# Six one-bank PSUM tiles instead of three two-bank tiles in the last stage of an attention and feed-forward kernel

## Chip, cores and metric

The kernel runs on one core of a Trainium2 chip. The metric is the time of one execution on the device in microseconds (us), and smaller is better. The engines are named as in the profile: PE (TensorE, matrix products), PEld (its weight loads), DVE (VectorE), ACT (ScalarE), POOL (GpSimd) and SP (SyncE, which only issues transfers here).

## What is computed

The inputs are q, k and v of 8 batches, 12 heads, 448 rows and 64 columns, and two weight matrices of 768 x 3072 and 3072 x 768. The attention uses a squared relu in place of a softmax:

```python
scores = scale * np.matmul(q, k.transpose(0, 1, 3, 2))
attn = np.maximum(scores, 0.0) ** 2 / S
x = np.matmul(attn, v)                      # heads side by side: 8 x 448 x 768
mixed = np.real(fft(fft(x, axis=1), axis=2))
u = x + mixed
un = (u - mu) / np.sqrt(var + 1e-06)        # over the 768 columns
out = u + np.maximum(un @ w_ch1, 0.0) @ w_ch2
```

## The kernel before

The 8 x 448 = 3584 rows of `un` are cut into twelve groups for the feed-forward part: groups of 384, 512 and 384 rows and then nine of 256. While the attention and the Fourier mixing of later batches still run, the first eight groups go through the feed-forward one at a time, between the other work (`ffn`, L1874). The last four groups come after all other work, in two pairs (`JOINTS`, L216): `joint` (L1733) takes two groups of 256 rows together and forms their first product by seven block products in place of eight (a scheme of Strassen's kind over two row halves and two halves of the 768 inner columns). The stage of the change is these two joints; in the profile it runs from 451.4 us to the end.

In a joint there are twelve blocks (`i`), and each has seven block products on PE. One block product is three matmuls of 256 columns (`product`, L1757, matmul at L1762), in a half of one PSUM bank. Three generators per block say in which order they come:

- `main` (L1786) takes one bank. It makes a product there, ACT copies the bank to SBUF (`copy`, L1777), PE adds a second product to the same bank, ACT copies it again, PE adds a third, ACT copies again, PE adds a fourth, and ACT's relu (L1806) writes the result to `hB`.
- `second` (L1810) takes one bank and makes one product. DVE adds the first copy and applies the relu (`sum_out`, L1782) into `hT`.
- `third` (L1819) takes one bank and makes one product. DVE adds the third copy (L1782, into `hB`), PE adds a last product, and DVE adds the second copy (L1782, into `hT`).

So a bank goes back and forth between PE and its readers, ACT and DVE, while other blocks use the other banks. The second product of the feed-forward (`Pair`, L2018) is a chain of matmuls of 384 columns (L2071), between which DVE adds a bank to the row block that will be stored (`adder`, L1623).

The order of all work is written by a planner while the program is built (`Streams.run`, L102): each generator asks for an engine with a duration, times of its inputs and free buffers, and the planner takes the request that can start first. The order on each engine is then fixed, and each engine works through its own queue in that order. What an instruction waits for is not written in the kernel. The layer below the kernel keeps a record per tile, and puts semaphore waits where an instruction touches a tile that another engine has used.

PSUM has eight banks here. `BF` (L238) makes two tiles of one bank, named `psF`. `BS` (L237) makes three tiles of two banks each, named `psS`; the attention needs both banks of such a tile in one instruction, since ACT reads the scores of two heads together (L967). In the last stage `spread` (L1708) takes the three wide tiles for good and hands out their six halves as single banks; two more come from `BF`. The eight are the pool `B8`:

```python
tiles, plain = [BS.take() for _ in range(3)], []
B8 = Banks(6, lambda i: tiles[i // 2][:, i % 2] if i < 6 else plain[i - 6])
```

Of the kernel before, what the change touches and what calls it, by code (L numbers as in the profile page):

```python
# [10 lines left out]
FP32 = mybir.dt.float32  # L11
# [138 lines left out]
def need(eng, dur, deps=(), bufs=(), ok=None):  # L150
    return eng, dur, list(deps), list(bufs), ok


def mm(n):
    return n / 2400 + (0.002 if STAGE[0] else 0.006)
# [22 lines left out]
def kernel(  # L178
# [10 lines left out]
    B, H, S, Dh = q.shape  # L189
# [33 lines left out]
    wpool = ctx.enter_context(tc.tile_pool(name="w", bufs=1))  # L223
    work = ctx.enter_context(tc.tile_pool(name="work", bufs=1))
    psum = ctx.enter_context(tc.psum_pool(name="ps", bufs=1))
    dram = ctx.enter_context(tc.tile_pool(name="dr", bufs=1, space=bass.MemoryType.DRAM))


# [5 lines left out]
    nbot = [dram.tile([UB, D], BF16, name=f"nbot{b}") for b in range(B)]  # L234


    BS = Banks(3, lambda i: psum.tile([128, 2, 512], FP32, name="psS", tag=f"S{i}", bufs=1))  # L237
    BF = Banks(2, lambda i: psum.tile([128, 512], FP32, name="psF", tag=f"F{i}", bufs=1))  # L238
    sch = Streams()
    STAGE[0] = 1  # L240
# [161 lines left out]
    def halve():  # L402

        yield need("SP", 0.0, [tail_left])
        e = yield need("PE", mm(2 * SX), [], [BS])
        pt = BS.take()
        for t in range(2):
# [4 lines left out]
        nc.vector.tensor_copy(half_seq[0][:2 * EH], pt[:2 * EH, :, 0:2 * EV].rearrange("p t (s o) -> p t o s", o=2))  # L412
        BS.give(pt, e)
        BQR.free.append(e)
# [397 lines left out]
    def turned_for(b, i):  # L812

        g, r = divmod(i, 7)
        return turned_at[b][g] if r == 3 else [turned_at[b][g][r > 3]]
# [18 lines left out]
    def attention(b, left=None):  # L834
# [8 lines left out]
        while pv < MC:  # L843
# [18 lines left out]
            if values:  # L862
                deps += [sv[i][1] for i in items(mv)]
                if b > 1:
                    yield need("PE", 0.0, deps, [], gate)
                    if chains[0] == 2:
                        homes, n = BS, min(n, 2)
                bufs.append(homes)
# [5 lines left out]
            if n:  # L874
                now = sorted(range(p, p + n), key=lambda i: i % 7 == 3)
                deps += [c for i in now for c in turned_for(b, i)]
                bufs += [BS] * n
                last = [sum(1 + (j % 7 == 3) for j in now[x + 1:]) * mm(S) for x in range(n)]
# [6 lines left out]
            for part in ("scores", "values") if few else ("values", "scores"):  # L885
                if part == "values" and values:
                    held = homes.take()
                    av = held[:, 0] if homes is BS else held
                    give = lambda when, homes=homes, held=held: homes.give(held, when)
# [747 lines left out]
    S_, Tk, hb, copies, ffn1_left = [None] * 5, [None] * 5, [], [], Cell()  # L1637
# [70 lines left out]
    def spread():  # L1708

        yield need("PE", 0.0, rows_mixed, [BS] * 3)  # L1710
        tiles, plain = [BS.take() for _ in range(3)], []
        B8 = Banks(6, lambda i: tiles[i // 2][:, i % 2] if i < 6 else plain[i - 6])

        def two_more():
            for i in (6, 7):
                e = yield need("SP", 0.0, [], [BF])
                plain.append(BF.take())
                B8.ids.append((e, i))
                B8.free.append(e)

        sch.add(two_more(), (0, 0))
        yield need("SP", 0.0, un_ready[B - 1])
        yield need("SP", 0.0, [], BU[0][1:] + BU[1][1:])
        for x in "", "1":
            t = work.tile([128, 3, 256], FP32, name="copies", tag=f"u{x}B", bufs=1)
            copies.append([t[:, n] for n in range(3)])
        yield need("SP", 0.0, [], [BTS, BUN[0]])
        ones = [work.tile([128, 256], FP32, name="copies", tag=t, bufs=1)
                for t in ("qs", "tp", "un0", "un1", f"pc{TC[0][0]}", f"pc{TC[1][0]}")]
        copies.extend((ones[0:3], ones[3:6]))  # L1730
        eight.extend((B8, Banks(4, lambda i: Set(copies[i]))))

    def joint(number):  # L1733
# [4 lines left out]
        if not eight:  # L1738
            yield from spread()
        B8, BK = eight  # L1740
        halves = hid[0].rearrange("p j n -> p (j n)").rearrange("p (x j n) -> p x j n", x=2, n=256)
# [44 lines left out]
        def main(i):  # L1786

            m1, u4 = Cell(), Cell()
            e = yield need("PE", d, [], [B8, BK])
            p, bk = B8.take(), BK.take()  # L1790
            cs = bk.aps
# [423 lines left out]
```

## Time and profile before

| | |
|---|---|
| time, median of 3 runs | 568.57 us (567.13 to 569.33) |
| profiled execution: span from its first to its last instruction | 566.4 us |
| profiled execution: its own time | not recorded apart from the span |
| PE busy over the span | 556.5 us (98%) |
| DVE / ACT / POOL busy | 436.2 / 318.2 / 195.9 us |
| granted TensorE clock | 1.000 |
| the stage of the change | 451.4 us to the end |

The runs' times hold a little more than the span: their median is 2.17 us above the span of the profiled execution. In the rows of the profile, L12 is line 12 of the kernel. A row of the timeline merges equal instructions that follow each other on an engine: its start, how long it lasts, the engine, line and operation, what it writes and reads, how many there are (x3), and in brackets the idle time of the engine before it with what ended that. The end of a matmul is modelled: a matmul of 256 columns is shown as 0.27 us long, but the next one may start earlier, so that two rows of PE can overlap. The rhythm of PE is therefore read from the starts.

### The profile page before, as it was taken

What the parts mean: (1) busy time and instruction counts of PE and PEld (TensorE: products, weight loads), DVE (VectorE), ACT (ScalarE), POOL (GpSimd) and SP (SyncE); (2) the same over time, 40 slices, a digit from 0 to 9 for tenths busy, and PEclk for the clock granted to TensorE, in tenths of its full rate; (3) what the DMA queues carried; (4) which work ended last, traced back from release to release, by engine and by line L of the source; (5) the groups of instructions that cost most, each with busy time, mean ns of one, the idle gap of its engine ahead of it and who ended that gap; (6) DMA issues with size and microseconds to landing.
All of it is one profiled execution on the core that took longest, in us unless ns stands there. A gap on an engine that the chain in (4) does not pass through costs nothing.

```text
span 566.4 us, 11147 instructions
## 1 busy us (share of the span) xinstructions
PE 556.5 (98%) x4171; PEld 350.1 (62%) x4171; DVE 436.2 (77%) x1016; ACT 318.2 (56%) x536; POOL 195.9 (35%) x281
## 2 busy tenths in 40 slices
PE   7999999999999999999999999999999999999997
PEld 4376556544465455556756757767678688668864
DVE  7976564987789978887997896888899957644762
ACT  5978762676745686585786637638515154015400
POOL 8966225523346234462545545222015000000000
PEclk9999999999999999999999999999999999999999
DMA  9999999979959988899899979956425421231012
GB/s 110 180 209 230 215 215 165 217 144 134 181 96 210 215 117 179 164 187 184 174 163 196 198 121 198 164 123 154 115 65 174 124 75 29 71 127 56 1 57 83
DMA packets 152688, 82.41 MB, mean 146 GB/s; under 512 B 118076, under 2 KB 147900, under 8 KB 152636
## 3 DMA queue, kind: packets, MB, share of 16 engines
q0 software_dynamic: 57056, 33.63, 43.0%
q1 hardware_dynamic: 95580, 48.09, 38.1%
q8 instruction: 32, 0.52, 0.4%
q14 instruction: 20, 0.16, 0.1%
HBM read 62.91 MB, written 26.25 MB: 157 GB/s over the span
## 4 chain that ended last, share of the span: by engine, by line
PE 86%; DMA 5%; DVE 4%; ACT 2%; POOL 1%; issue 1%; DVEq 0%; POOLq 0%; ACTq 0%
PE psF L1930 25%; PE psF L2071 20%; PE psS L1762 8%; PE psS L954 7%; PE psS L2071 5%; DMA kn<-in_k_dram 5%; PE psF L827 5%; PE psF L1985 4%; PE psS L1432 2%; PE psF L1762 2%; PE psF L1958 2%; PE psF L822 1%; PE psF L623 1%; DVE sq L984 1%; PE psS L827 1%
## 5 line engine op out<-in xcount | busy, mean ns | idle before, releaser
L1930 PE MATMUL psF<-unT,w 128*128 128x256 bf16 (+2 forms) x1152 | 165.3, 299 | 0.0
L967 ACT ACTIVATE sq<-psS 128x896 bf16<-128x896 f32 x168 | 144.1, 919 | 31.7 <-PE psS L954 31.2
L1930 PEld LDWEIGHTS <-w 128*128 128x128 bf16 x1152 | 110.9, 98 | 49.6 <-issue 5.2
L984 DVE TENSOR_TENSOR sq<-sq 128x896 bf16<-128x896 bf16 x144 | 88.9, 634 | 13.3 <-ACT sq L967 12.5
L2071 PEld LDWEIGHTS <-hT 128*128 128x128 bf16 x648 | 62.5, 98 | 44.1 <-issue 4.8
L1917 ACT ACTIVATE hT<-psF 128x512 bf16<-128x512 f32 (+2 forms) x121 | 59.6, 508 | 41.1 <-PE psF L1930 40.3
L1623 DVE TENSOR_TENSOR o<-psF,o 128x384 f32<-128x384 f32 (+1 forms) x78 | 42.6, 547 | 24.3 <-PE psF L2071 20.8
L2071 PE MATMUL psF<-w,hT 128*128 128x384 bf16 x336 | 59.7, 326 | 0.6 <-DVE o L1623 0.6
L954 PE MATMUL psS<-qkT 64*128 64x448 bf16 (+1 forms) x336 | 51.5, 354 | 1.0 <-DVE qkT L630 0.8
L1777 ACT COPY copies<-psS 128x256 f32<-128x256 f32 x57 | 19.9, 374 | 53.0 <-PE psS L1762 48.1
L689 DVE TENSOR_SCALAR xT<-psF 128x224 bf16<-128x224 f32 x60 | 20.6, 384 | 26.1 <-PE psF L827 26.1
L1275 POOL TENSOR_TENSOR u<-tp,xn 112x385 f32<-112x385 f32 (+2 forms) x14 | 14.5, 1037 | 72.6 <-DVE tp L1255 48.6
L476 POOL DMA_DIRECT2D qn<-in_q_dram x21 | 15.7, 747 | 57.7 <-DVE qkr L583 50.3
L827 PE MATMUL psF<-sq,vn 128*64 128x448 bf16 x246 | 33.0, 362 | 0.0
L954 PEld LDWEIGHTS <-qkT 64*128 64x128 bf16 (+1 forms) x336 | 12.9, 94 | 32.3 <-issue 26.4
L1762 PEld LDWEIGHTS <-w 128*128 128x128 bf16 x288 | 28.2, 98 | 4.7 <-issue 1.1
L451 POOL DMA_DIRECT2D kn<-in_k_dram x42 | 25.9, 626 | 10.3 <-DMA w<-in_moe_w_ch_dram 6.0
L1284 DVE BATCH_NORM_STATS2 stats<-u 112x6 f32<-112x384 f32 (+2 forms) x56 | 28.7, 543 | 0.8 <-POOL u L1275 0.6
L451 POOL DMA_DIRECT2D vn<-in_v_dram x42 | 26.1, 638 | 6.2 <-DMA w<-in_moe_w_ch_dram 5.4
L476 POOL DMA_DIRECT2D vn<-in_v_dram x24 | 18.9, 789 | 25.5 <-PE psS L954 25.4
L1303 ACT ACTIVATE un<-u,small 112x768 bf16<-112x768 f32 (+2 forms) x22 | 22.0, 1023 | 9.5 <-DVE small L1290 8.4
L1782 DVE CUSTOM_DVE_ANT_0 hT<-psS,copies 128x256 bf16<-128x256 f32 x37 | 15.0, 421 | 14.1 <-PE psS L1762 6.2
(238 smaller groups left out, 946.9 us busy)
## 6 DMA issues: line engine op xcount, KB each, us to landing
out_dram<-o SPq DMA_DIRECT2D x55, 192.0 KB, 2.3
qn<-in_q_dram POOLq DMA_DIRECT2D x21, 224.0 KB, 5.1
vn<-in_v_dram POOLq DMA_DIRECT2D x24, 192.0 KB, 5.6
w<-in_moe_w_ch_dram POOLq DMA_DIRECT2D x12, 384.0 KB, 11.8
w<-in_moe_w_ch_dram POOLq DMA_DIRECT2D x4, 1152.0 KB, 23.4
kn<-in_k_dram POOLq DMA_DIRECT2D x21, 192.0 KB, 5.9
utop<-u SPq DMA_DIRECT2D x12, 336.0 KB, 2.9
o<-utop SPq DMA_DIRECT2D x16, 192.0 KB, 3.7
```

The source lines that it names most:

```text
L451: nc.gpsimd.dma_start(out=t[par * Dh:(par + 1) * Dh, par::2], in_=at)
L476: nc.gpsimd.dma_start(out=to, in_=src[b, hs, 0:rows].rearrange("h (p j) d -> p h (j d)", j=j))
L827: nc.tensor.matmul(av[h * Dh:(h + 1) * Dh, 0:S], lhsT=vn_home[:, at:at + Dh], rhs=sq[:, h, :], start=start, stop=stop, skip_group_check=True)
L954: nc.tensor.matmul(sc[:, h, 0:S].rearrange("k (c q) -> k c q", c=4), lhsT=flat[ps, k0:k0 + KB], rhs=qT[ps, pair], start=True, stop=True)
L967: nc.scalar.activation(r, sc[:, :, 0:S], AF.Relu)
L984: nc.vector.tensor_tensor(r, r, r, op=ALU.mult)
L1284: nc.vector.bn_stats(stats[:n, hf, :], u[:n, hf * (D // 2):(hf + 1) * (D // 2)])
L1623: nc.vector.tensor_tensor(o[:, cols], pc[:, cols], o[:, cols], op=ALU.add)
L1762: nc.tensor.matmul(ps[:, 0:N], lhsT=lhs, rhs=rhs[:, m], start=(start and m == 0), stop=(stop and m == 2), skip_group_check=True)
L1917: nc.scalar.activation(hs, ps, AF.Relu)
L1930: nc.tensor.matmul(ph[:, i * N:(i + 1) * N], lhsT=w1_sb[m][hf][:, (jj + i) * 128:(jj + i + 1) * 128], rhs=unT[:, m, 0:N], start=(m == 0), ...
L2071: nc.tensor.matmul(pc[:, cols], lhsT=lhs[i], rhs=rhs[i][:, cols], start=(start and i == 0), stop=(i == KP - 1), skip_group_check=True)
```

## The change

The three wide tiles get a PSUM pool of their own (`wide`), which the attention uses as before. When the last stage begins, `spread` closes that pool and opens another one, `p1`, in the same room. Each time `B8` hands out one of its first six banks, it makes a new tile of one bank there, with one of six tags. The two banks from `BF` stay as they were. Where the names of the lists would collide, one is renamed.

```diff
     psum = ctx.enter_context(tc.psum_pool(name="ps", bufs=1))
+    wide = tc.psum_pool(name="pw", bufs=1)
+    wide_psum = wide.__enter__()
...
-    BS = Banks(3, lambda i: psum.tile([128, 2, 512], FP32, name="psS", tag=f"S{i}", bufs=1))
+    BS = Banks(3, lambda i: wide_psum.tile([128, 2, 512], FP32, name="psS", tag=f"S{i}", bufs=1))
     BF = Banks(2, lambda i: psum.tile([128, 512], FP32, name="psF", tag=f"F{i}", bufs=1))
...
         yield need("PE", 0.0, rows_mixed, [BS] * 3)
-        tiles, plain = [BS.take() for _ in range(3)], []
-        B8 = Banks(6, lambda i: tiles[i // 2][:, i % 2] if i < 6 else plain[i - 6])
+        plain = []
+        wide.__exit__(None, None, None)
+        ones = ctx.enter_context(tc.psum_pool(name="p1", bufs=1))
+        B8 = Banks(6, lambda i: ones.tile([128, 512], FP32, name="psS", tag=f"one{i}", bufs=1) if i < 6 else plain[i - 6])
```

Lines of this stage stand four lower in the changed kernel: L1762, L1777, L1782, L1806 and L2071 become L1766, L1781, L1786, L1810 and L2075.

Apart from line numbers and buffer numbers, the built programs hold the same instructions in the same order on every engine. What differs, in this stage alone, are the waits. Of the block products' 504 matmuls 103 hold a wait before and 137 after. Where an instruction needs more waits than it can hold, a small instruction that only waits is put ahead of it; of those DVE has 21 more and ACT 14 more.

The first place is ACT's queue at the start of the first joint: the copies of `copy`. In brackets stand the semaphores that a row waits for (PE_49, DVE_49 and Activation_49 count what these engines have finished, the DMA ones count transfers). Before:

```order
L1777 COPY copies<-psS 128x256 [waits PE_49]
L1777 COPY copies<-psF 128x256 [waits DMASW1_49,PE_49]
L1777 COPY copies<-psS 128x256 [waits DVE_49,PE_49] x2
L1777 COPY copies<-psS 128x256 [waits DVE_49]
L1777 COPY copies<-psF 128x256 [waits PE_49]
```

After:

```order
L1781 COPY copies<-psS 128x256 [waits PE_49]
L1781 COPY copies<-psF 128x256 [waits DMASW1_49,PE_49]
L1781 COPY copies<-psS 128x256 [waits PE_49] x3
L1781 COPY copies<-psF 128x256 [waits PE_49]
L1781 COPY copies<-psS 128x256 [waits PE_49] x2
```

Three copies that waited for DVE (for its reading of the other half of the same wide tile) wait for PE alone.

The second place is DVE's queue at the start of the second joint: the sums of `sum_out` (shown as ISA here and as CUSTOM_DVE_ANT_0 in the profile). Before:

```order
L1782 ISA hT<-psS,copies 128x256 [waits PE_49,Activation_49]
L1782 ISA hT<-psS,copies 128x256 [waits Activation_49] x2
L1782 ISA hT<-psF,copies 128x256 [waits PE_49,Activation_49]
L1782 ISA hB<-psS,copies 128x256 [waits PE_49,Activation_49] x2
L1782 ISA hB<-psS,copies 128x256 [waits Activation_49]
L1782 ISA hT<-psS,copies 128x256
L1782 ISA hB<-psF,copies 128x256 [waits PE_49,Activation_49]
```

After:

```order
L1786 ISA hT<-psS,copies 128x256 [waits PE_49,Activation_49] x3
L1786 ISA hT<-psF,copies 128x256 [waits PE_49,Activation_49]
L1786 ISA hB<-psS,copies 128x256 [waits PE_49,Activation_49] x3
L1786 ISA hT<-psS,copies 128x256 [waits PE_49]
L1786 ISA hB<-psF,copies 128x256 [waits PE_49,Activation_49]
```

The order is the same, and every sum now names its own product and its own copy. The count that a wait asks for does not show in these rows; read from the built programs, the second of the two `hB` sums (the sixth of these rows' nine instructions) asks in the program before for a product that stands five block products later on PE than its own, in the other half of its wide tile.

More of the change, by code (lines that the diff above doesn't have):

```diff
@@ L1727, in spread @@
         yield need("SP", 0.0, [], [BTS, BUN[0]])
-        ones = [work.tile([128, 256], FP32, name="copies", tag=t, bufs=1)
+        singles = [work.tile([128, 256], FP32, name="copies", tag=t, bufs=1)
                 for t in ("qs", "tp", "un0", "un1", f"pc{TC[0][0]}", f"pc{TC[1][0]}")]
-        copies.extend((ones[0:3], ones[3:6]))
+        copies.extend((singles[0:3], singles[3:6]))
         eight.extend((B8, Banks(4, lambda i: Set(copies[i]))))
```

## Prediction

> **What bounds the kernel now.** I read the page first: how busy is each engine over the span, and at which clock does PE run?
>
> ```profile
> span 566.4 us, 11147 instructions
> PE 556.5 (98%) x4171; PEld 350.1 (62%) x4171; DVE 436.2 (77%) x1016; ACT 318.2 (56%) x536; POOL 195.9 (35%) x281
> PEclk9999999999999999999999999999999999999999
> ```
>
> PE is busy for 98% of the span, at the full granted clock in every slice. The share is an average, so the stage of the change is read by itself: first joint until its block products end, the second products of that joint, the same two stretches of the second joint, and the tail.
>
> ```profile
> core 0: us, PE busy (x) PEld busy (x) DVE busy (x) ACT busy (x) POOL busy (x), PEclk, DMA share, GB/s
> 451.40:484.70 33.30, 33.30 (x288) 28.00 (x287) 22.41 (x59) 16.32 (x48) 0.00 (x0) 1.00 0.20 59
> 484.70:506.60 21.90, 21.90 (x137) 13.20 (x135) 11.78 (x30) 0.00 (x0) 0.00 (x0) 1.00 0.32 97
> 506.60:542.50 35.90, 35.37 (x299) 29.05 (x298) 21.68 (x59) 16.29 (x48) 0.00 (x0) 1.00 0.14 41
> 542.50:562.60 20.10, 20.04 (x136) 12.68 (x133) 8.70 (x20) 0.00 (x0) 0.00 (x0) 1.00 0.26 88
> 562.60:566.40 3.80, 0.00 (x0) 0.00 (x0) 0.60 (x2) 0.00 (x0) 0.00 (x0) 1.00 0.17 53
> ```
>
> In 111.2 us PE is shown idle for 0.59 us, while ACT has 17.0 us and DVE 10.9 us to spare in the first stretch alone. But a busy PE need not be a PE at its own rhythm, since the modelled end of a matmul covers short stalls. The chain that ended last gives the rhythm: long stretches in which one matmul follows another.
>
> ```profile
> 417.73 2.00 PE psS L1432 x24
> 427.58 10.48 PE psF L1930 x96
> 454.33 0.98 PE psS L1762 x9
> 552.76 1.95 PE psF L2071 x12
> ```
>
> A matmul of 256 columns takes 10.48 / 96 = 0.109 us before the stage, and 0.98 / 9 = 0.109 us in it; one of 384 columns takes 1.95 / 12 = 0.1625 us. The first stretch by itself has these numbers of the two kinds:
>
> ```profile
> 451.40:484.70 33.30, 28.32 (x252) 24.66 (x252) 1.00 0.20 59
> 451.40:484.70 33.30, 6.29 (x36) 3.35 (x35) 1.00 0.20 59
> ```
>
> 252 x 0.109 + 36 x 0.1625 = 27.5 + 5.8 = 33.3 us, which is the whole stretch, to within a stall of 0.15 us found below. So this stage is bound by PE working at its own rhythm, and the question for the change is how many stalls there are to take away.
>
> **Where PE stalls.** I went through the timeline of PE and looked for starts that are further apart than three matmuls, 0.33 us (two: 0.22 us). There are four:
>
> ```profile
> 475.61 0.49 PE L1762 MATMUL psS<-unT,w 128*128 128x256 bf16 x3
> 476.09 0.27 PE L1762 MATMUL psS<-unT,quarter 128*128 128x256 bf16 x1
> ...
> 513.39 0.49 PE L1762 MATMUL psS<-unT,quarter 128*128 128x256 bf16 x3
> 513.72 0.49 PE L1762 MATMUL psF<-unT,quarter 128*128 128x256 bf16 x3
> 514.04 0.49 PE L1762 MATMUL psF<-chan,w 128*128 128x256 bf16 x3
> 514.83 0.81 PE L1762 MATMUL psS<-sumx,w 128*128 128x256 bf16 x6 [0.30 <-DVE hT L1782]
> ...
> 522.47 0.38 PE L1762 MATMUL psS<-chan,xT 128*128 128x256 bf16 x2
> 522.89 0.49 PE L1762 MATMUL psS<-sumx,w 128*128 128x256 bf16 x3
> ...
> 535.45 0.38 PE L1762 MATMUL psS<-chan,xT 128*128 128x256 bf16 x2
> 536.02 0.49 PE L1762 MATMUL psS<-chan,w 128*128 128x256 bf16 x3 [0.19 <-DVE hT L1782]
> ```
>
> The rows at 513.39, 513.72 and 514.04 show the steady step of 0.33 us. The losses are 0.48 - 0.33 = 0.15, 0.79 - 0.33 = 0.46, 0.42 - 0.22 = 0.20 and 0.57 - 0.22 = 0.35 us: together 1.16 us. A smaller fifth one, of 0.02 us at 532.56, is left out.
>
> **What the change removes.** With a record per wide tile, an access to one half waits for what was issued before on the other half. These are the rows of the readers at the four stalls:
>
> ```profile
> 474.88 0.37 ACT L1777 COPY copies<-psS 128x256 f32<-128x256 f32 x1 [1.75 <-PE psS L1762]
> 475.62 0.42 DVE L1782 CUSTOM_DVE_ANT_0 hB<-psS,copies 128x256 bf16<-128x256 f32 x1
> ...
> 511.68 0.65 ACT L1777 COPY copies<-psS 128x256 f32<-128x256 f32 x2 [0.66 <-PE psS L1762]
> 512.05 0.43 DVE L1782 CUSTOM_DVE_ANT_0 hB<-psS,copies 128x256 bf16<-128x256 f32 x1 [1.51 <-ACT copies L1777]
> 513.69 0.76 DVE L1782 CUSTOM_DVE_ANT_0 hB<-psS,copies 128x256 bf16<-128x256 f32 x2 [1.21 <-PE psS L1762]
> 514.36 0.41 DVE L1782 CUSTOM_DVE_ANT_0 hT<-psS,copies 128x256 bf16<-128x256 f32 x1
> ...
> 520.65 1.30 ACT L1777 COPY copies<-psS 128x256 f32<-128x256 f32 x4 [0.66 <-PE psS L1762]
> 522.01 0.42 DVE L1782 CUSTOM_DVE_ANT_0 hB<-psS,copies 128x256 bf16<-128x256 f32 x1 [1.84 <-ACT copies L1777]
> 522.47 0.37 ACT L1777 COPY copies<-psS 128x256 f32<-128x256 f32 x1 [0.51 <-DVE hB L1782]
> ...
> 535.21 0.76 DVE L1782 CUSTOM_DVE_ANT_0 hT<-psS,copies 128x256 bf16<-128x256 f32 x2 [1.27 <-PE psS L2071]
> ```
>
> I followed each stall back with the waits of both built programs.
>
> At 476.09 the product adds to a bank that ACT has copied by 474.88 + 0.37 = 475.25, but in the program before it also waits for the DVE sum on the other half, which ends at 475.62 + 0.42 = 476.04. Without that wait the product is free at its turn: 0.15 us.
>
> At 514.83 PE waits for the sum at 514.36, which ends at 514.77. That sum stands in DVE's queue behind the one at 513.69, which is held for 1.21 us by a product in the other half. Its own product was done before that: its copy, the last of the two at 511.68, ends at 512.33. With its own waits alone it can start when DVE is free, at about 512.5, and the three sums behind one another end near 513.6, before PE's turn at 514.37: 0.46 us.
>
> At 522.89 PE waits for the copy at 522.47, held by the sum at 522.01 on the other half. In the changed program PE needs the sum itself, which needs a copy that ends at about 521.3 (the second of the four from 520.65); it can end at 521.3 + 0.42 = 521.7, before PE's turn at 522.69: 0.20 us.
>
> At 536.02 PE waits for the second sum of 535.21, delayed with the first one by 1.27 us because a matmul of L2071 uses the other half. In the changed program this product has no wait of its own left: 0.35 us.
>
> The sum is 1.16 us, all of it on the path, since PE has no other idle time up to 562.6 and everything behind follows PE. What is late next is PE's own rhythm: the readers, ahead of PE before, get further ahead. Nothing in the other 450 us changes, since instructions, order and waits are the same there, and the tail of 3.80 us stays.
>
> **What the change adds.** It adds 34 waits to matmuls of the block products. A wait that is already fulfilled could cost nothing, or it could cost the overlap of two matmuls, 0.27 - 0.11 = 0.16 us, which gives 34 x 0.16 = 5.4 us; no reason makes it a gain. I take 0: 103 of these matmuls wait already, and the first stretch, with about half of them, equals its matmuls times the undisturbed rhythm.
>
> More products also report their end: 59 more counts in the built program, one per product. The trace shows that stretches of L1762, which change banks after three matmuls, have the 0.109 us of L1930, which does so after twelve. The starts are rounded to 0.01 us, so the rows could hide 0.02 us per product at most, 59 x 0.02 = 1.2 us; no reason makes a count a gain. I take 0, by the equal rhythms. Here the Trainium skill speaks against the change: "TensorE: Matmul & The Clock Gate", section "The cost: per-tile semaphore tail", says that completion counts of matmuls that run together come one after another at about 26 ns each, by which, as an estimate from that page, 59 more would cost 1.6 us and turn the sum into a loss of 0.4 us. The equal rhythms show no such price.
>
> It adds 21 small waiting instructions to DVE's queue and 14 to ACT's. At the price of a whole sum (0.42 us) and a whole copy (0.37 us) they would be 8.8 and 5.2 us, beside 10.9 + 14.2 us of idle DVE and 17.0 + 19.6 us of idle ACT in the first and third stretch; at least they cost nothing. Behind them queue sums and copies for which PE waits, and if a hundredth of a microsecond of each reached PE it would be 0.35 us. I take 0, since PE waits at four places only.
>
> Closing one pool and opening another could hold the first products until all readers of the wide tiles are done. The last product of earlier work in such a tile is at 417.73 (L1432), 32 us before the stage, so it costs 0. The banks also get other numbers; no row shows a bank's number, psF and psS products step alike above, and I take 0.
>
> Sum: 566.4 - 1.16 = 565.2 us of span, and from the median of 568.57 us a time of **567.4 us**.
>
> **The rivals.**
>
> *The stalls are handed on* (chance 0.12). A product freed from one wait reaches the next of its chain earlier and stalls there. For it: both joints are chains of product, copy, product. Against it: DVE and ACT lose waits too and have the idle time above. Half the gain would remain: 568.0 us.
>
> *The gain is lost* (0.09). Either waits merge again below the kernel, so that the separate tiles separate nothing, or the counts take their bound of 1.2 us. Against the first: the lists of waits differ. Against the second: the equal rhythms. Both give 568.6 us.
>
> *Slower, by drained matmuls* (0.04). Each of the 34 added waits lets the matmul before it run out: 5.4 - 1.16 gives 572.8 us. It decides above (2.84 + 1.16) / 34 = 0.12 us per wait. Against it: the rows at 513.39 to 514.04 and the first stretch.
>
> *Faster by more than the stalls* (0.05). The order is fixed and PE keeps its rhythm, so more than 1.2 us cannot come from this stage; it would need work elsewhere that the rows do not show, or the spread of the runs, 567.13 to 569.33 us: 565.5 us.
>
> **How the numbers follow.** The forecast has the other 0.70. One half of one per cent is 2.84 us, about what a measurement of this kernel can tell from no change. The forecast, the handed-on stalls and the lost gain all lie within that: 0.91 for the same, 0.05 for faster, 0.04 for slower. The range reaches up from the forecast by the bounds of the unknown costs, 567.4 + 1.2 + 0.35 = 569.0 us, which takes in both cases without a gain, and down by the distance of the fastest run from the median, 568.57 - 567.13 = 1.4 us, to 566.0 us.
>
> **What would show it.** In the trace after, PE's starts in the two joints are nowhere more than 0.33 us apart between products of three; idle PE between 451 and 562 us falls from 0.59 us to under 0.1; the sum that started at 513.69 starts about 1.2 us earlier; the tail after the last matmul stays at 3.8 us. I am wrong if new gaps stand in PE's timeline, if the rhythm of L1766 rises above 0.109 us, or if the time moves by over 2.84 us either way.

## The result, and the profile after

Over 20 runs of each, the kernel before has a median of 567.93 us (566.92 to 570.51) and the changed kernel 566.61 us (565.78 to 568.94). The ratio is 0.9976, with a 95% interval of 0.9965 to 0.9987: between 0.7 and 2.0 us less, 1.3 us in the middle. That is a real gain, and it is smaller than the half of one per cent that the prediction called the same. The profiled execution took 566.29 us, with a span of 564.5 us.

The page of the changed kernel reads as before at first sight:

```profile
span 564.5 us, 11177 instructions
...
PE 555.8 (98%) x4166; PEld 350.2 (62%) x4171; DVE 437.5 (77%) x1016; ACT 319.8 (57%) x536; POOL 196.3 (35%) x281
...
PEclk9999999999999999999999999999999999999999
```

The span is 1.9 us shorter, and the shares do not tell why. The windows of the changed kernel over the same five stretches (each boundary moved with the work) do:

```profile
core 0: us, PE busy (x) PEld busy (x) DVE busy (x) ACT busy (x) POOL busy (x), PEclk, DMA share, GB/s
450.69:483.84 33.15, 33.15 (x288) 28.01 (x287) 22.87 (x59) 17.26 (x48) 0.00 (x0) 1.00 0.22 59
483.84:505.74 21.90, 21.90 (x137) 13.20 (x135) 11.78 (x30) 0.00 (x0) 0.00 (x0) 1.00 0.32 97
505.74:541.10 35.36, 35.36 (x302) 29.36 (x301) 22.76 (x60) 17.00 (x48) 0.00 (x0) 1.00 0.14 42
541.10:560.70 19.60, 19.55 (x133) 12.38 (x130) 8.26 (x20) 0.00 (x0) 0.00 (x0) 1.00 0.26 90
560.70:564.50 3.80, 0.00 (x0) 0.00 (x0) 0.61 (x2) 0.00 (x0) 0.00 (x0) 1.00 0.17 53
```

The first stretch lost the 0.15 us of its one stall, and PE has no idle time left in the third. The tail is the same 3.80 us. To compare whole stages I take the window from the start of the first block product to the end of the last matmul; this is its row, before and after:

```profile
451.55:562.54 110.99, 110.46 (x853) 82.84 (x851) 64.41 (x165) 32.60 (x96) 0.00 (x0) 1.00 0.21 65
```

```profile
450.84:560.65 109.81, 109.81 (x853) 82.86 (x851) 65.51 (x165) 34.27 (x96) 0.00 (x0) 1.00 0.22 66
```

The stage is 110.99 - 109.81 = 1.18 us shorter, for the same matmuls. In the changed one PE is shown busy for all of it. A busy PE can hide short stalls, so the steps from start to start count: in the trace after, over the 852 matmuls of the stage (the windows' 853 count one that began before it), every step is 0.109 to 0.110 us after a matmul of 256 columns and 0.162 to 0.163 us after one of 384. The stage also begins 0.71 us earlier, 450.84 against 451.55 us. That difference is there before the stage: one wait of PE, 350 us ahead of it, makes nearly all of it. The rows around that wait, before and after:

```profile
92.16 9.91 PE L1958 MATMUL psF<-w,hT 128*128 128x384 bf16 x60
103.04 0.51 PE L1205 MATMUL psS<-ident,un 128*128 128x128 bf16 x6 [0.97 <-ACT un L1303]
```

```profile
92.10 9.91 PE L1962 MATMUL psF<-w,hT 128*128 128x384 bf16 x60
102.33 0.51 PE L1207 MATMUL psS<-ident,un 128*128 128x128 bf16 x6 [0.32 <-ACT un L1305]
```

The two profiles are 0.06 us apart at the first row and 0.71 us at the second, and the programs do the same work there.

At the four places of the stalls, the timeline of PE after:

```profile
474.90 0.49 PE L1766 MATMUL psS<-unT,w 128*128 128x256 bf16 x3
475.23 0.27 PE L1766 MATMUL psS<-unT,quarter 128*128 128x256 bf16 x1
...
512.85 0.49 PE L1766 MATMUL psF<-unT,quarter 128*128 128x256 bf16 x3
513.18 0.49 PE L1766 MATMUL psF<-chan,w 128*128 128x256 bf16 x3
513.51 0.82 PE L1766 MATMUL psS<-sumx,w 128*128 128x256 bf16 x6
...
521.15 0.38 PE L1766 MATMUL psS<-chan,xT 128*128 128x256 bf16 x2
521.37 0.49 PE L1766 MATMUL psS<-sumx,w 128*128 128x256 bf16 x3
...
533.91 0.38 PE L1766 MATMUL psS<-chan,xT 128*128 128x256 bf16 x2
534.12 0.49 PE L1766 MATMUL psS<-chan,w 128*128 128x256 bf16 x3
```

Every step is now 0.33 us after three matmuls and 0.21 to 0.22 us after two. The reason stands in DVE's queue, here around the second stall:

```profile
511.19 0.42 DVE L1786 CUSTOM_DVE_ANT_0 hB<-psS,copies 128x256 bf16<-128x256 f32 x1 [0.56 <-ACT copies L1781]
512.17 0.42 DVE L1786 CUSTOM_DVE_ANT_0 hB<-psS,copies 128x256 bf16<-128x256 f32 x1 [0.56 <-ACT hB L1810]
512.73 0.42 DVE L1786 CUSTOM_DVE_ANT_0 hT<-psS,copies 128x256 bf16<-128x256 f32 x1
```

The `hB` sum that was the first of the two at 513.69, 7.18 us after the second joint's first product (506.51), now starts at 511.19, 5.54 us after it (505.65). That is 1.64 us earlier, more than the 1.2 us that I had expected, since the sum ahead of it in DVE's queue is earlier too (at 510.21 us, 4.56 us after the first product, where it was 512.05 - 506.51 = 5.54 us). Its row no longer names a product of PE behind an idle time; it waits for its copy (ACT, L1781). The sum for which PE waited ends at 512.73 + 0.42 = 513.15, and PE's turn is at 513.51.

Who waited for whom in the stage, before (rows not shown above) and after:

```profile
ACT copies L1777 <- DVE hT L1782: 4.1, 7, 0.8
...
ACT hB L1806 <- DVE hB L1782: 0.6, 1, 0.6
ACT copies L1777 <- DVE hB L1782: 0.5, 1, 0.5
PE psS L1762 <- DVE hT L1782: 0.5, 2, 0.3
```

```profile
ACT copies L1781 <- PE psS L1766: 47.2, 35, 22.8
```

(Each row gives the sum of the waits in us, how many there were, and the longest.) ACT's nine waits for DVE, 5.2 us in all, and PE's two are gone from the view after, and ACT's copies wait for PE, which makes what they copy.

### The profile page after: what moved, and what is told of

Same layout as the page of the kernel before. It is cut to its first block, busy times and chain, and to the rows that moved or that the text cites. A ratio compares the mean times of both kernels' runs of the same rounds, so it can differ in the third digit from the quotient of the medians.

```text
span 564.5 us, 11177 instructions
## 1 busy us (share of the span) xinstructions
PE 555.8 (98%) x4166; PEld 350.2 (62%) x4171; DVE 437.5 (77%) x1016; ACT 319.8 (57%) x536; POOL 196.3 (35%) x281
## 4 chain that ended last, share of the span: by engine, by line
PE 88%; DVE 4%; DMA 3%; ACT 2%; issue 1%; POOL 1%; DVEq 0%; POOLq 0%; ACTq 0%
PE psF L1934 26%; PE psF L2075 20%; PE psS L1766 8%; PE psS L956 8%; PE psS L2075 5%; PE psF L829 5%; PE psF L1989 4%; DMA kn<-in_k_dram 3%; PE psF L1766 2%; PE psS L1434 2%; PE psF L1962 2%; PE psF L824 1%; PE psF L625 1%; DVE sq L986 1%; PE psS L829 1%
## 5 line engine op out<-in xcount | busy, mean ns | idle before, releaser
L986 DVE TENSOR_TENSOR sq<-sq 128x896 bf16<-128x896 bf16 x144 | 89.0, 635 | 13.2 <-ACT sq L969 12.2
L2075 PEld LDWEIGHTS <-hT 128*128 128x128 bf16 x648 | 62.5, 98 | 44.1 <-issue 4.8
L2075 PE MATMUL psF<-w,hT 128*128 128x384 bf16 x336 | 59.7, 326 | 0.6 <-DVE o L1625 0.6
L1781 ACT COPY copies<-psS 128x256 f32<-128x256 f32 x57 | 20.5, 372 | 47.2 <-PE psS L1766 47.2
L691 DVE TENSOR_SCALAR xT<-psF 128x224 bf16<-128x224 f32 x60 | 20.6, 384 | 26.3 <-PE psF L829 26.2
L1766 PEld LDWEIGHTS <-w 128*128 128x128 bf16 x288 | 28.2, 98 | 3.7
L829 PEld LDWEIGHTS <-vn 128*64 128x64 bf16 x288 | 12.5, 108 | 21.1 <-issue 17.5
```

The source lines that it names most:

```text
L829: nc.tensor.matmul(av[h * Dh:(h + 1) * Dh, 0:S], lhsT=vn_home[:, at:at + Dh], rhs=sq[:, h, :], start=start, stop=stop, skip_group_check=True)
L986: nc.vector.tensor_tensor(r, r, r, op=ALU.mult)
L1766: nc.tensor.matmul(ps[:, 0:N], lhsT=lhs, rhs=rhs[:, m], start=(start and m == 0), stop=(stop and m == 2), skip_group_check=True)
L2075: nc.tensor.matmul(pc[:, cols], lhsT=lhs[i], rhs=rhs[i][:, cols], start=(start and i == 0), stop=(i == KP - 1), skip_group_check=True)
```

## The experiments

In each the order of instructions on every engine is that of the kernel before; banks, tiles and waits differ. The stage is always the window from the first block product to the end of the last matmul.

**The pool apart, nothing else.** Against the kernel before:

```diff
+    wide_psum = ctx.enter_context(tc.psum_pool(name="pw", bufs=1))
...
-    BS = Banks(3, lambda i: psum.tile([128, 2, 512], FP32, name="psS", tag=f"S{i}", bufs=1))
+    BS = Banks(3, lambda i: wide_psum.tile([128, 2, 512], FP32, name="psS", tag=f"S{i}", bufs=1))
```

> The wide tiles get a pool of their own, but the last stage keeps using their halves as before. Instructions, order and waits are those of the kernel before; only the bank numbers differ (the two one-bank tiles are opened first and stand in other banks). Theory (the gain is the waits on the other half): the four stalls are there again, the stage from the first block product to the last matmul lasts 111.0 us as before, and the time is that of the kernel before, within 0.1%. Rival (the other bank numbers make part of the gain, namely the 0.71 us by which the stage began earlier in the profile after, 450.84 against 451.55 us): the stage begins near 450.8 us and the time is about 0.7 us, 0.12%, below the kernel before.

Measured: 567.63 us, a ratio of 1.0001 with an interval of 0.9987 to 1.0015. Its stage, and one of its stalls:

```profile
451.31:562.30 110.99, 110.47 (x854) 82.81 (x851) 64.33 (x165) 32.60 (x96) 0.00 (x0) 1.00 0.22 65
```

```profile
513.81 0.49 PE L1763 MATMUL psF<-chan,w 128*128 128x256 bf16 x3
514.59 0.38 PE L1763 MATMUL psS<-sumx,w 128*128 128x256 bf16 x2 [0.29 <-DVE hT L1783]
```

The stage has the 110.99 us of before to the hundredth, with the stall of 0.78 - 0.33 = 0.45 us in its place. To this stage the bank numbers and the separate pool by itself are worth nothing. The stage began at 451.31 us, between the 451.55 us of before and the 450.8 us of the rival, and the rival's 0.12% is just inside the interval of the time. What decides against it is the place where the 0.71 us arose, 350 us ahead of the stage, as shown above.

**Only the third pair split.** Against the changed kernel; the first two pairs stay wide:

```diff
+        joined = {k: ones.tile([128, 2, 512], FP32, name="psS", tag=f"two{k}", bufs=1) for k in (0, 1)}
...
+            if i // 2 in joined:
+                return joined[i // 2][:, i % 2]
+            return ones.tile([128, 512], FP32, name="psS", tag=f"one{i}", bufs=1)
```

> Two of the three pairs of banks stay two-bank tiles in the last stage; only the third pair is split into one-bank tiles. The stalls at 514.83, 522.89 and 536.02 us come from waits on the other half of the third tile (the last one by way of DVE's queue), the one at 476.09 us from the first tile. Theory: these three stalls go and the one of 0.15 us stays; the stage lasts 111.0 - 1.0 = 110.0 us. Rival (stalls are handed on to other products as soon as some are freed): new gaps in PE's starts, a stage of 110.3 us or more. Rival (the gain belongs to the pool, not to the split): no stalls are left in the stage, 109.8 us.

Measured, in one run: 565.94 us. The stage, and the place of the stall that should stay:

```profile
450.30:560.28 109.98, 109.98 (x853) 82.82 (x851) 64.50 (x165) 32.85 (x96) 0.00 (x0) 1.00 0.22 66
```

```profile
474.36 0.49 PE L1775 MATMUL psS<-unT,w 128*128 128x256 bf16 x3
474.84 0.27 PE L1775 MATMUL psS<-unT,quarter 128*128 128x256 bf16 x1
```

110.99 - 109.98 = 1.01 us = 0.46 + 0.20 + 0.35, as expected. The step of 0.48 us is there as before. Note the window's row: PE looks busy for all 109.98 us, although it stalls; only the starts show it.

**Only the first two pairs split.** The same edit with `(2,)` in place of `(0, 1)`.

> The complement: the first and the second pair are split, the third pair stays a two-bank tile. Theory: the stall at 476.09 us (0.15 us) and the one at 536.02 us (0.35 us) go, those of 0.46 and 0.20 us stay; the stage lasts 111.0 - 0.5 = 110.5 us. Rival (handed on): the stage stays above 110.7 us with gaps at other places. Rival (pool, not split): 109.8 us.

Measured, in one run: 568.37 us. The stage, and the stall that should stay:

```profile
451.23:561.70 110.47, 110.14 (x854) 82.84 (x851) 64.27 (x165) 33.28 (x96) 0.00 (x0) 1.00 0.22 66
```

```profile
513.58 0.49 PE L1775 MATMUL psF<-chan,w 128*128 128x256 bf16 x3
514.36 0.49 PE L1775 MATMUL psS<-sumx,w 128*128 128x256 bf16 x3 [0.29 <-DVE hT L1795]
```

110.99 - 110.47 = 0.52 us, the 0.15 + 0.35 us that were expected and the 0.02 us left out of the sum. The 0.35 us go in either run, as was expected, so together the two runs make 1.01 + 0.52 - 0.35 = 1.18 us, the whole gain. The stalls follow the tiles, and removing one does not move it to another place: the first rival of the prediction, the stalls handed on, falls here. By the time of this one run, 568.37 us, the kernel would seem slower than before; the stage says otherwise. Here the tail behind the last matmul was longer too, 566.6 - 561.7 = 4.9 us, against 566.4 - 562.5 = 3.9 us before; why is not known.

**One tile of all six banks.** Against the changed kernel:

```diff
+        six = ones.tile([128, 6, 512], FP32, name="psS", tag="six", bufs=1)
+        B8 = Banks(6, lambda i: six[:, i] if i < 6 else plain[i - 6])
```

> The opposite direction: one tile of six banks in the last stage, so that an access to any of the six waits for what was issued before on any other. Instructions and order are the same. Theory (waits on neighbours in a tile are what costs): PE has to wait before many of the 168 block products; at 0.03 to 0.2 us for each the stage grows by 5 to 34 us. Rival (the readers have so much time to spare that only a few products are ever held): the stage grows by less than 2 us.

Measured, in one run: 631.01 us. The stage, and PE's waits in it:

```profile
451.89:624.78 172.89, 124.34 (x854) 82.79 (x851) 65.68 (x165) 33.53 (x96) 0.00 (x0) 0.99 0.14 42
```

```profile
PE psS L1767 <- DVE hT L1787: 14.6, 22, 1.2
PE psS L1767 <- ACT copies L1782: 13.1, 26, 1.1
PE psS L1767 <- DVE hB L1787: 8.9, 13, 1.0
```

172.89 - 110.99 = 61.9 us: the direction was expected, the size not. I had put a price of 0.03 to 0.2 us on each of 168 products; these three rows alone come to 36.6 us in 61 waits, 0.6 us each. A held product holds the readers behind it, and these hold the next product, as at this place:

```profile
457.69 0.42 DVE L1787 CUSTOM_DVE_ANT_0 hT<-psS,copies 128x256 bf16<-128x256 f32 x1 [0.77 <-PE psS L1767]
458.15 0.92 ACT L1782 COPY copies<-psS 128x256 f32<-128x256 f32 x3 [1.87 <-DVE hT L1787]
459.12 0.49 PE L1767 MATMUL psS<-chan,quarter 128*128 128x256 bf16 x3 [1.14 <-ACT copies L1782]
```

DVE's sum ends at 458.11, ACT's three copies run from 458.15 to 459.07, and PE goes on at 459.12: the readers' whole turns stand on the path, one behind the other.

**Two tiles of three banks.** Against the changed kernel:

```diff
+        threes = [ones.tile([128, 3, 512], FP32, name="psS", tag=f"three{k}", bufs=1) for k in range(2)]
+        B8 = Banks(6, lambda i: threes[i // 3][:, i % 3] if i < 6 else plain[i - 6])
```

> Two tiles of three banks in the last stage, so that each bank has two neighbours (one before, none in the changed kernel, five in the run with one tile of six banks, where the stage grew by 61.9 us to 172.9 us). Order and instructions are the same. Theory (PE pays only where the held readers fall behind its turn, so the price grows faster than the number of neighbours): more than 1.2 x 2 = 2.4 us over the stage of the changed kernel, 109.8 us, and well under 2/5 of what six banks cost; 113 to 130 us. Rival (a fixed price per neighbour, 1.2 us each): 112.2 us.

Measured, in one run: 578.77 us, with a stage inside the 113 to 130 us that were expected.

```profile
451.07:573.09 122.02, 114.91 (x853) 82.38 (x851) 64.30 (x165) 32.07 (x96) 0.00 (x0) 1.00 0.20 59
```

With none, one, two and five neighbours for each of the six banks, the stage is 0, 1.2, 12.2 and 63.1 us longer than 109.81 us. A fixed price per neighbour is out.

**Six tiles kept.** Against the changed kernel, the one-bank tiles are made once:

```diff
+        kept = [ones.tile([128, 512], FP32, name="psS", tag=f"one{i}", bufs=1) for i in range(6)]
+        B8 = Banks(6, lambda i: kept[i] if i < 6 else plain[i - 6])
```

> As the changed kernel, but the six one-bank tiles are made once when the stage begins and handed out again and again, in place of a new tile at each take. Theory (separate records are what counts): no stalls, a stage of 109.8 us and a time 0.2 to 0.3% below the kernel before. Rival (the fresh tile at each take is needed, since an old record drags waits along): some of the four stalls come back, 110.0 us or more.

Measured: 566.4 us, a ratio of 0.9982, with an interval of 0.9957 to 1.0006 from fewer runs.

```profile
450.57:560.38 109.81, 109.81 (x853) 82.83 (x851) 65.47 (x165) 34.30 (x96) 0.00 (x0) 1.00 0.22 66
```

The timing does not tell it from no change, but the stage does: 109.81 us. A fresh tile at each take is not needed.

**Any bank, and the same once more.** Against the changed kernel, `self.pool.take(e)` in the chains of the second product becomes `self.pool.take()`, at two places. The same kernel was run a second time.

> As the changed kernel, but the chains of the second product take the bank that was free first, without looking whether its former neighbour is in use, since there are no neighbours any more. Theory (PE's own rhythm of 0.109 and 0.1625 us per matmul is the floor of the stage, and it is reached): 109.8 us, no less. Rival (the choice of banks still costs or hides something): a stage shorter or longer by 0.3 us or more.

Measured, in one run: 569.28 us. The stage lasts what it should, but it begins 3 us late:

```profile
453.82:563.63 109.81, 109.81 (x854) 82.86 (x851) 65.45 (x165) 34.26 (x96) 0.00 (x0) 1.00 0.22 66
```

The timeline of PE in this run has two idle times between 86 and 114 us that the run with the six kept tiles has not:

```profile
91.37 2.11 PE L1962 MATMUL psF<-w,hT 128*128 128x384 bf16 x12 [1.19 <-DMA w<-in_moe_w_ch_dram]
105.33 0.51 PE L1207 MATMUL psS<-ident,un 128*128 128x128 bf16 x6 [0.77 <-ACT un L1305]
```

> The kernel that takes any free bank, once more and timed in rounds. Its single look gave 569.28 us although its stage lasted 109.81 us; the stage began at 453.82 us, against 450.3 to 451.9 us in the other runs, whose work ahead of the stage is the same. Theory (the start of the stage varies from run to run): a median within 0.1% of the changed kernel's share of the kernel before, that is 0.2 to 0.3% below it, and a stage of 109.81 us wherever it begins. Rival (the other choice of banks delays the work ahead of the stage): the stage begins near 453.8 us again and the median is 0.2% or more above the kernel before.

Measured: 566.7 us, a ratio of 0.9984 with an interval of 0.997 to 0.9998, 0.16% below the kernel before: a little less than expected, with an interval that holds the 0.2 to 0.3%.

```profile
450.87:560.68 109.81, 109.81 (x853) 82.87 (x851) 65.50 (x165) 34.27 (x96) 0.00 (x0) 1.00 0.22 66
```

So the late start was that run's alone. The ten profiles, whose work ahead of the stage is the same, begin it at 450.3 to 453.8 us, whichever tiles they use. The 0.71 us between the profiles before and after is a difference of this kind, not a part of the gain.

## Why the prediction was right

The forecast of 567.4 us stood on the median of three runs, 568.57 us; with twenty runs that median is 567.93 us, and the same sum from there gives 566.8 us. Measured are 566.61 us. The difference of 1.32 us agrees with the 1.16 us of the sum within its interval, 0.7 to 2.0 us.

*What bounds the stage.* Right. Without its stalls the stage is 109.81 us long in four profiles of three kernels (the changed one, the six kept tiles and, twice, any bank), to the hundredth. That is the sum of the steps given above, without a gap. PE's rhythm is the floor, and the chain that ended last shows it unchanged in the changed kernel:

```profile
453.62 0.98 PE psS L1766 x9
```

*The four stalls.* Right in place and size: 1.01 us for three of them together and, with the fifth, 0.52 us for two, against 1.01 and 0.50 us. All five, with the 0.02 us left out, make 1.18 us, and the stage is 1.18 us shorter.

*How the second stall goes.* Right in its end, wrong in one step. I let the three sums end near 513.6 us, 0.77 us before PE's turn. I had overlooked that the last of them needs its own product, which PE ends only at 513.55 us, in the times of the program before:

```profile
513.06 0.49 PE L1762 MATMUL psS<-sumx,w 128*128 128x256 bf16 x3
```

After the change the sum ends 513.51 - 513.15 = 0.36 us ahead of PE. The margin is half of what I wrote, and was enough.

*What the change adds.* Taken as 0, and the sum leaves no room for more: 110.99 - 1.18 = 109.81 us is the measured stage, so 34 more waits, 59 more counts and 35 more small waiting instructions together cost the stage no more than the rounding, about 0.02 us. One reading behind the 0 for the new pool was wrong: the last product of earlier work in a wide tile is not the one at 417.73 us. In the trace before, L1240 uses these tiles from 421.5 to 427.3 us, and the last reader of its products, DVE at L1257, ends at 429.6 us. The tiles are free 22 us ahead of the stage and not 32; the 0 stands.

The price that the Trainium skill gives in "TensorE: Matmul & The Clock Gate", section "The cost: per-tile semaphore tail", does not appear here: 26.3 ns for each of 59 counts would be 1.6 us, by an estimate from that page. The section speaks of matmuls that run together in parts of the array; here they follow each other.

*The rivals.* Stalls handed on: refuted by the two partial splits. The gain lost: refuted by the stage. Drained matmuls: refuted by the rhythm. Faster by more than the stalls: the 1.9 us by which the profiled span is shorter would have suggested it, but 0.71 us of that lie ahead of the stage and belong to the spread of the runs.

## What to carry to other kernels

Waits are kept per tile: banks that are used one by one want a tile each. Here the price of shared tiles grew steeply with their banks, from 1.2 us with two banks in a tile over 12.2 us with three to 63.1 us with six. What such false waits are worth is read from the starts of the bounding engine, not from its busy share and not from the readers' idle time: ACT alone had waited 5.2 us for DVE here, and PE had lost 1.18 us. For a gain smaller than the spread of the runs, compare the length of the stage in single profiles: it repeated to 0.01 us here, 110.99 us in two profiles with the tiles of before and 109.81 us in four without stalls.

## What was not expected

A stall of PE up to the overlap of two matmuls, 0.27 - 0.11 = 0.16 us, does not show as idle time: the profile before gave 0.53 us of idle PE in its stage, where the starts gave 1.18 us, and the run with the third pair split shows a fully busy PE that still loses 0.15 us.

The spread of the runs arises early. Compared with the run of the six kept tiles, the run that began its stage at 453.82 us is 1.1 us late after 20 us of the span and 3.3 us late from 111 us on, and then stays so, to 0.03 us, through the 340 us up to the stage. Of its two rows above, one shows PE waiting for a transfer of weights and the other for ACT, at the place where the profiles before and after part too. Between 70 and 112 us DVE waited 6.9 us for the transfer of q where it waited 4.4 us in the other run; what delays these from run to run was not tried.
